# Attention scores exponentiated in PSUM instead of in a moved SBUF row, with the freed SBUF given to three load rings

## The chip, the cores and the metric

The kernel runs on one core of one Trainium2 chip. The metric is the device time of one execution in microseconds, as the median of several executions. Beside it there is one profiled execution with its own time and trace, from which all durations below come.

## What is computed

The outputs of two independent layers are put side by side: a 32-head softmax attention (A) and an FNet mixing layer (B), both over 2048 tokens of width 1024, all in float32.

```python
qkv = (x @ wqkv).reshape(B, S, 3, H, Dh)          # H = 32 heads, Dh = 32
scores = einsum("bhqd,bhkd->bhqk", q, k) * Dh ** -0.5
p = softmax(scores, axis=-1)
A = einsum("bhqk,bhkd->bhqd", p, v) -> [B, S, D] @ wo
a = einsum("bsd,ed->bse", x, dft_hid_re);  b = einsum("bsd,ed->bse", x, dft_hid_im)
B = einsum("ts,bse->bte", dft_seq_re, a) - einsum("ts,bse->bte", dft_seq_im, b)
return concatenate([A, B], axis=-1)
```

## The kernel before, in words

**Two kinds of TensorE work are interleaved.** The first is the dense products: the query, key and value projections, the two stages of B, and the output projection. Each is computed by a seven-product scheme of block additions, and each operand is split into a rounded part and a remainder, so that one product becomes three matmuls of 128 x 128 by 128 x 512. Such matmuls are called "fills" in the code. They are made in `group` (line 398). Their operands pass through rings of SBUF buffers: `RAW` (loaded tiles), `GR` (a second loaded term that is added or subtracted), `HR` and `LR` (the rounded part and the remainder of a stationary piece, tags `h` and `l`), and numbered slots for moving pieces. `fetch` loads and adds (lines 446, 455, 462), `halves` splits (lines 482, 483, 486).

The second kind is attention, in three streams for each head h:

- **S**: 32 score tiles of 128 queries by 1024 keys. Each is two matmuls into one `psS` tile of PSUM (line 1204). The tile is used only for the row's minimum of the negated scores and for the row's sum of exponentials. For h = 0, VectorE takes the negated maximum from PSUM (`tensor_reduce`, line 1214), and ScalarE exponentiates in PSUM, in place, with an accumulated sum (line 1220). For every other head, VectorE copies the negated scores to a row buffer `srow` in SBUF while it takes the minimum (`tensor_scalar` with an accumulated output, line 1212), and ScalarE exponentiates that row in SBUF (line 1218). `srow` has NROW = 2 buffers of 4 KB in each partition.
- **T**: when all S tiles of a head are done, its row minimum is written as two more rows of the query operand (through two small DMAs), and the scores are computed again, transposed and already shifted: 64 matmuls of 128 x 512 into `psT` (line 1335), each followed by a ScalarE exponential into SBUF (line 1339).
- **V**: three blocks of matmuls for each head, after 5, 10 and 16 of its 16 key blocks (`ENDS`), which multiply the exponentials by the values (line 1354).

PSUM has room for two `psS` tiles, two `psT` tiles and two `psD` (`pd`) tiles, the last for fills and V. The rings `psS_r` and `psT_r` say who must be done before a tile is written again: in `scores`, for h > 0, the list `users` of a `psS` tile holds the matmuls and the VectorE operation `b`, while the ScalarE operation `e` belongs to `ruse`, the list of the row buffer. For h = 0 both are in `users`.

**The order of all engines is fixed by a planner** inside the kernel. It plays the program through with a cost for each operation (`MOVE` 1.23, `MAX` 1.22, `ES` 1.31 for the S exponential, `ET` 0.64 for the T exponential, and so on) and emits instructions in that order; each engine's queue then runs in order on the chip. At each free moment of TensorE it chooses: a V block before the others (held back by at most `PATIENCE` 0.5 while an S or T matmul is about to be ready, or while ScalarE has less than `STOCK` 1.8 of work), then S and T, where S may run ahead of T by at most `LEAD`; if none of these is ready, or attention is ahead of its share, the next fill (line 1468). An attention matmul counts as ready `LATE` (0.25; `SLATE`, also 0.25, for S) after the planned end of what it waits for, on top of a latency of 0.1. On ScalarE, T exponentials go before S exponentials; on VectorE, the S operation goes before most of the dense work, the evacuations of the value blocks excepted.

**Stages.** Up to some 180 us there are only fills, whose loads use a ring of raw buffers of their own (`ahead`, line 604, 10 buffers tagged `er`). Attention then runs beside the fills until shortly after 2770 us. The output projection (`behind`, `project`) comes last: it needs the attention output of all heads, its first load waits for the last head's store (list `over`), and its loads use rings of their own, 9 raw tiles and 5 second terms (line 1070), in SBUF that attention has given up.

Of the kernel before, what the change touches and what calls it, by code (L numbers as in the profile page):

```python
# [8 lines left out]
F32 = mybir.dt.float32  # L9
F32R = mybir.dt.float32r  # L10
AF = mybir.ActivationFunctionType
ALU = mybir.AluOpType
# [4 lines left out]
P = 128  # L17
# [5 lines left out]
NS = S // P  # L23
NB = 512
NPT = 24
NROW = 2
NE = 4
NLOW = 5
ENDS = (0, 5, 10, 16)
# [188 lines left out]
def kernel(  # L218
# [114 lines left out]
    def att_low():  # L333

        att()
        return late["atl"]
# [5 lines left out]


    MM, PV, SWITCH, TINY = 0.2272, 0.86, 0.30, 0.17
    ES, ET = 1.31, 0.64
    MOVE = 1.23
    MAX, EVAC, CAST, BIT = 1.22, 0.685, 0.415, 0.275
    SUB = 1.31
    ISSUE = 0.46

    LATE, SLATE = 0.25, 0.25
    HB = 0
    ACAST = 0.63
    RES = 400
# [47 lines left out]
                k += 1  # L402
        frees.append(finish(lambda: box["ps"], o))

    RAW, HR, LR, GR, ER = Ring(5), Ring(3), Ring(3), Ring(3), Ring(NE)
    slots = [[] for _ in range(40)]

    def take_slot(i):
# [83 lines left out]
    def piece(terms, store=None):  # L492

        box = {}
        raw, made, users = fetch([P, 4, P], terms, store)
        (o0, u0), (o1, u1) = HR.take(), LR.take()

        def tile_of(key):
            def get():
                if key not in box:  # L500
                    box[key] = parts.tile([P, 4, P], F32R, name=key, tag=key, bufs=3)
                return box[key]
            return get

        h, l = tile_of("h"), tile_of("l")
        made = halves(raw, made, users, h, l, (o0, o1), (u0, u1), (HR, LR))
        both = Both(u0, u1)
        return Piece(h, l, made, both)
# [66 lines left out]
    def qkv():  # L575
# [25 lines left out]
            }[p]()  # L601

        XS, WV, X, u3 = {}, {}, {}, {}
        ahead = (Ring(10), RAW, lambda shape, name, n: vp.tile(shape, F32, name="er", bufs=10) if name == "raw" else pre.tile(shape, F32, name="raw", tag="raw", bufs=5), [])
        within = where[0]

        def load_x(x, k):
# [458 lines left out]
    def behind():  # L1066

        over.extend(o for h in o_st for o in h)
        for i in range(20, 28):
            slots[i] = list(over)  # L1070
        where[0] = (Ring(9), Ring(5), lambda shape, name, n: op_pool().tile(shape, F32, name=name, tag=name, bufs=n), over)
        spare[0] = True

    over = []
# [91 lines left out]
    psS_r, psT_r, pt_r, vt_r, rt_r, ot_r = Ring(2), Ring(2), Ring(NPT), Ring(2), Ring(1), Ring(2)  # L1166
    small = {n: Ring(b) for n, b in (("st", 2), ("nm", 2), ("lh", 2), ("tw", 1))}
    qx_r = Ring(1)
    row_r = Ring(NROW)
    got = {}  # L1170
    Tops, Sops = {}, {}
    exp_of = {}
# [5 lines left out]
    def scores(h):  # L1178
        ST = {}
        sold, suse = small["st"].take()  # L1180
        maxes, exps = [], []
        if h:
            xold, xuse = qx_r.take()

            def load_x():
                att()
                g, r0 = divmod(h, 4)
                nc.sync.dma_start(f(QX[0])[0 : 3 * DH], qk_d[2 * g][0][r0 * DH : r0 * DH + DH].rearrange("d i c -> (d i) c"))

            got[h, "x"] = op("SP", ISSUE, load_x, [*xold, *qk_st[2 * (h // 4)][0], *(att_gate if h == 1 else [])], [xuse], -2, 192)  # L1190
        for n, (qt, c) in enumerate([(k % 4, k // 4) for k in range(8)] + [divmod(k, 2) for k in range(8, 32)]):
            old, users = psS_r.take()
            own = h > 0 and qt < 4
            box = {}
            if h:
                rold, ruse = row_r.take()

            def mm(n=n, qt=qt, c=c, box=box, own=own):
                if n == 0:
                    ST["negm"] = sm.tile([P, 2, NS], F32, name="negm", bufs=2)  # L1200
                    ST["sums"] = sm.tile([P, 2, NS], F32, name="sums", bufs=2)
                box["p"] = p = psS.tile([P, 1024], F32, name="psS")
                for i in range(2):
                    nc.tensor.matmul(  # L1204
                        p[:, i * NB : i * NB + NB], (QX[0] if own else QS[h % 2])[:, qt * P : qt * P + P],
                        KS[h % 2][:, c * 1024 + i * NB : c * 1024 + i * NB + NB], start=True, stop=True,
                    )

            def mx(qt=qt, c=c, box=box):
                if h:  # L1210
                    box["s"] = att_low().tile([P, 1024], F32, name="srow", bufs=NROW)
                    nc.vector.tensor_scalar(box["s"], box["p"], -1.0, None, op0=ALU.mult, op1=ALU.min, accum_out=ST["negm"][:, c, qt : qt + 1])  # L1212
                    return
                nc.vector.tensor_reduce(out=ST["negm"][:, c, qt : qt + 1], in_=box["p"], axis=AX.X, op=ALU.max, negate=True)

            def ex(qt=qt, c=c, box=box):
                if h:
                    nc.scalar.activation(box["s"], box["s"], AF.Exp, scale=-1.0, bias=ST["negm"][:, c, qt : qt + 1], accum_out=ST["sums"][:, c, qt : qt + 1])  # L1218
                    return
                nc.scalar.activation(box["p"], box["p"], AF.Exp, bias=ST["negm"][:, c, qt : qt + 1], accum_out=ST["sums"][:, c, qt : qt + 1])  # L1220

            a = op("PE", 2 * MM, mm, [*old, *([got.get((h, "x"))] if own else [got.get((h, 0, qt // 4)), got.get((h, "z"))]), got.get((h, 1, 2 * c)), got.get((h, 1, 2 * c + 1))],
                   [users, xuse] if own else [users])
            b = op("DVE", MOVE if h else MAX, mx, [a] + (sold if n == 0 else []) + (rold if h else []), [users, suse, *([ruse] if h else [])], 0)
            e = op("ACT", ES, ex, [b], [ruse if h else users, suse], 0)
            exp_of[a] = e
            maxes.append(b)
            exps.append(e)
            Sops.setdefault(h, []).append(a)
            streams["S"].append((a, h, n))  # L1230
            if n == 5 and h:
                sums(h - 1)

        nold, nuse = small["nm"].take()
        lold, luse = small["lh"].take()
        box = {}

        def nmin():
            ST["nm"] = sm.tile([P, NS], F32, name="nm", bufs=2)
            nc.vector.tensor_reduce(out=ST["nm"], in_=ST["negm"].rearrange("p c n -> p n c"), axis=AX.X, op=ALU.min)  # L1240

        def high():
            box["l"] = sm.tile([P, 2, NS], F32R, name="lh", bufs=2)
            nc.vector.tensor_reduce(out=box["l"][:, 0], in_=ST["negm"].rearrange("p c n -> p n c"), axis=AX.X, op=ALU.min)

        def low():
            return nc.vector.tensor_tensor(out=box["l"][:, 1], in0=ST["nm"], in1=f(box["l"])[:, 0], op=ALU.subtract)

        b = op("DVE", TINY, high, maxes + lold, [luse, suse], -2)
        a = op("DVE", TINY, nmin, maxes + nold, [nuse, suse], -2)  # L1250
        c = op("DVE", TINY, low, [a, b], [nuse, luse], -2, two=True)
        def across():
            box["t"] = sm.tile([P, 2 * NS], F32, name="lt", bufs=2)
            nc.vector.transpose(box["t"], f(box["l"]).rearrange("p i s -> p (i s)"))

        d = op("DVE", TINY, across, [b, c], [luse], -2)

        put = op("SP", ISSUE, lambda: nc.sync.dma_start(m_d[h].rearrange("i (g p) -> g i p", g=4), box["t"]), [d], [luse], -3, 32)
        moved = [op("SP", ISSUE, lambda: nc.sync.dma_start(f(QS[h % 2])[96:98, :], m_d[h].rearrange("(i q) p -> i (q p)", i=2)), [put], [], -3, 16)]
        mine[h] = (ST, suse, nuse, exps, moved)  # L1260
# [154 lines left out]
    while nf < len(fills) or any(place[n] < len(s) for n, s in streams.items()):  # L1415
# [18 lines left out]
        for n, (o, h, k) in heads.items():  # L1434
            if o.left:
                continue
            ready = o.ready + (SLATE if n == "S" else LATE)
            if n == "V":
                ready = max(ready, room)
            if ready > pl.now:  # L1440
                times.append(ready)
                continue
            if n == "V":

                near = any(m in heads and heads[m][0].left == 0 and heads[m][0].ready + LATE < pl.now + NEAR and not (m == "S" and held) for m in "ST")
                if (near or stock < STOCK) and pl.now < o.ready + PATIENCE:
                    times.append(o.ready + PATIENCE)
                    continue
            rank = {"V": 0, "T": 1, "S": 0.5 if stock > SFIRST else 1.5}[n]
            if n == "S" and "T" in heads and heads["T"][0].left == 0:  # L1450
                th, tk = heads["T"][1:]
                lead = k / 33.0 * SST + 16 * (h - th - 1) - tk / 4
                if lead > LEAD:
                    continue
                if lead > 0:
                    rank = 2
            ok.append((rank, n))
# [67 lines left out]
```

## Time and profile before

| what | value |
|---|---|
| median of 3 executions | 2960.72 us (2960.04 to 2961.28) |
| the profiled execution, its own time | 2957.99 us |
| its span, from the first to the last instruction | 2956.1 us |
| mean granted TensorE clock | 1.0 |
| DMA, mean over the span | 189 GB/s |
| last S matmul starts at | 2689.7 us |

How to read the lines shown below: a group's row gives line, engine, operation, tile written <- tiles read, shapes and count, then the busy time in us and the mean duration of one in ns, then the engine's idle time just before and what ended it. A row of the timeline gives start and duration in us, then the instruction and how many of its kind were merged (x2), and in brackets the idle time before it and what ended it. Matmuls are pipelined and their ends are modelled, so the distance between two starts says more than a matmul's duration. A row of the windows gives the stretch, its length, and then busy time and count of PE, PEld (weight loads), DVE (VectorE), ACT (ScalarE) and POOL (GpSimd), the granted clock, the DMA share and GB/s.

### The profile page before, as it was taken

To read this page: it belongs to the slowest core of one execution; us is meant where nothing else is said; L and a number is where in the kernel's file an instruction comes from. 1 tells how busy PE (TensorE), PEld (TensorE's weight loads), DVE (VectorE), ACT (ScalarE), POOL (GpSimd) and SP (SyncE) were. 2 spreads that over 40 slices of the span, in tenths; PEclk is the share of its full clock that TensorE was granted. 3 is DMA by queue.
4 is the path that set the end of the run, shared out by engine and by line. 5 is a ranking of instruction groups with operands and counts; after the bars stand their busy time and mean duration, and the time that the engine had idled before them with its cause. 6 is when DMAs were issued, how large, how long until landed. Compare 5 with 4: busy or idle time off the path is not lost.

```text
span 2956.1 us, 45723 instructions
## 1 busy us (share of the span) xinstructions
PE 2940.3 (99%) x14912; PEld 2145.2 (73%) x14912; DVE 2345.2 (79%) x4198; ACT 2300.3 (78%) x4314; POOL 860.8 (29%) x672
## 2 busy tenths in 40 slices
PE   9999999999999999999999999999999999999999
PEld 7887677776777777777777777777777777677787
DVE  6779788688877877787778888888777888887585
ACT  4348888888898888888888888898888888887421
POOL 2313236222212322221112343332112443442142
PEclk9999999999999999999999999999999999999999
DMA  9975669666626655554535775555434775565662
GB/s 350 355 231 165 191 186 300 215 213 232 205 64 198 206 151 160 174 180 146 155 93 162 229 242 154 174 161 161 118 109 135 238 250 175 167 179 177 233 220 104
DMA packets 376581, 558.59 MB, mean 189 GB/s; under 512 B 111100, under 2 KB 111100, under 8 KB 376220
## 3 DMA queue, kind: packets, MB, share of 16 engines
q1 hardware_dynamic: 376344, 555.68, 59.6%
q8 instruction: 118, 1.93, 0.3%
q14 instruction: 119, 0.97, 0.1%
HBM read 402.42 MB, written 153.11 MB: 188 GB/s over the span
## 4 chain that ended last, share of the span: by engine, by line
PE 98%; DVE 1%; ACT 1%; DMA 0%; POOL 0%; issue 0%; SPq 0%; DVEq 0%; POOLq 0%
PE pd L398 44%; PE psT L1335 16%; PE psS L1204 16%; PE pd L1354 15%; PE psT L398 7%; DVE srow L1212 1%; ACT srow L1218 0%; ACT pt L1339 0%; DMA er<-in_xa 0%; DMA g<-in_ct 0%; DVE h L483 0%; POOL slot L486 0%; POOL l L486 0%; ACT ptl L1339 0%; DVE l L486 0%
## 5 line engine op out<-in xcount | busy, mean ns | idle before, releaser
L1212 DVE TENSOR_SCALAR_CACHE_REDUCE srow<-psS 128x1024 f32<-128x1024 f32 x992 | 1203.2, 1220 | 168.3 <-ACT srow L1218 135.3
L1218 ACT ACTIVATE srow<-srow,negm 128x1024 f32<-128x1024 f32 x992 | 1198.2, 1216 | 6.8 <-DVE srow L1212 6.6
L398 PE MATMUL pd<-slot,h 128*128 128x512 f32 x3384 | 1169.9, 390 | 0.5 <-DVE h L483 0.5
L1339 ACT ACTIVATE pt<-psT 128x512 f32<-128x512 f32 x1618 | 925.9, 645 | 262.3 <-PE psT L1335 226.9
L1335 PE MATMUL psT<-qs,ks 128*128 128x512 f32 x2048 | 793.7, 394 | 1.7 <-ACT pt L1339 1.5
L398 PEld LDWEIGHTS pd<-slot,h 128*128 128x128 f32 x3384 | 635.2, 188 | 136.5 <-issue 1.7
L398 PE MATMUL pd<-slot,l 128*128 128x512 f32 x1692 | 659.6, 390 | 0.9 <-POOL l L486 0.7
L1335 PEld LDWEIGHTS psT<-qs,ks 128*128 128x128 f32 x2048 | 381.5, 188 | 139.4 <-issue 42.8
L1204 PE MATMUL psS<-ks,qs 128*128 128x512 f32 x1552 | 470.4, 391 | 1.0 <-DVE srow L1212 0.8
L486 POOL TENSOR_TENSOR l<-raw,h 128x512 fp32r<-128x512 f32 x152 | 197.2, 1297 | 758.9 <-DVE h L483 349.6
L1354 PE MATMUL pd<-pt,vt 128*32 128x512 f32 x3236 | 394.5, 594 | 0.0
L462 POOL TENSOR_TENSOR raw<-raw,g 128x512 f32<-128x512 f32 x211 | 273.0, 1300 | 376.5 <-DVE raw L462 96.2
L398 PEld LDWEIGHTS pd<-slot,l 128*128 128x128 f32 x1692 | 317.6, 188 | 69.2 <-POOL l L486 1.6
L1204 PEld LDWEIGHTS psS<-ks,qs 128*128 128x128 f32 x1552 | 290.5, 188 | 64.8 <-DVE srow L1212 3.0
L1339 ACT ACTIVATE ptl<-psT 128x512 f32<-128x512 f32 x430 | 249.0, 641 | 106.1 <-PE psT L1335 90.1
L486 POOL TENSOR_TENSOR slot<-raw,slot 128x512 fp32r<-128x512 f32 x154 | 199.0, 1298 | 380.9 <-DVE l L486 97.6
L1218 ACT ACTIVATION_READ_ACCUMULATOR srow<-srow,negm 128x1 f32 x992 | 259.7, 262 | 0.0
L1354 PEld LDWEIGHTS pd<-pt,vt 128*32 128x32 f32 x3236 | 102.0, 110 | 187.4 <-issue 177.3
L398 PE MATMUL pd<-slot,slot 128*128 128x512 f32 x768 | 194.7, 390 | 0.0
L483 DVE CAST h<-raw 128x512 fp32r<-128x512 f32 x321 | 146.6, 458 | 25.9 <-PE pd L398 19.2
L398 PEld LDWEIGHTS pd<-slot,slot 128*128 128x128 f32 x768 | 144.2, 188 | 31.0
L1354 PE MATMUL pd<-ptl,vt 128*32 128x512 f32 x860 | 164.2, 595 | 0.0
(126 smaller groups left out, 2262.6 us busy)
## 6 DMA issues: line engine op xcount, KB each, us to landing
raw<-in_ct SPq DMA_DIRECT2D x224, 256.0 KB
g<-in_ct SPq DMA_DIRECT2D x128, 256.0 KB
qk_d<-e SPq DMA_DIRECT2D x52, 512.0 KB
qs<-qk_d SPq DMA_DIRECT2D x128, 192.0 KB
ks<-qk_d SPq DMA_DIRECT2D x128, 192.0 KB
raw<-ab_d SPq DMA_DIRECT2D x96, 256.0 KB
c<-u_d SPq DMA_DIRECT2D x88, 256.0 KB
g<-ab_d SPq DMA_DIRECT2D x80, 256.0 KB
```

The source lines that it names most:

```text
L398: nc.tensor.matmul(box["ps"], a[1]((a[0].hi, a[0].lo)[u]()), b[1]((b[0].hi, b[0].lo)[v]()), start=k == 0, stop=k == n - 1)
L462: return (nc.gpsimd if e == "POOL" else nc.vector).tensor_tensor(out=dest(), in0=dest() if a is None else a.get(), in1=other["q"] if "q" i ...
L483: return nc.vector.tensor_copy(hi(), raw())
L486: return (nc.gpsimd if e == "POOL" else nc.vector).tensor_tensor(out=lo(), in0=raw(), in1=f(hi()), op=ALU.subtract)
L1204: nc.tensor.matmul(p[:, i * NB : i * NB + NB], (QX[0] if own else QS[h % 2])[:, qt * P : qt * P + P], KS[h % 2][:, c * 1024 + i * NB : c * ...
L1212: nc.vector.tensor_scalar(box["s"], box["p"], -1.0, None, op0=ALU.mult, op1=ALU.min, accum_out=ST["negm"][:, c, qt : qt + 1])
L1218: nc.scalar.activation(box["s"], box["s"], AF.Exp, scale=-1.0, bias=ST["negm"][:, c, qt : qt + 1], accum_out=ST["sums"][:, c, qt : qt + 1])
L1335: nc.tensor.matmul(box["p"], KS[h % 2][:, t * P : t * P + P], QS[h % 2][:, j * NB : j * NB + NB], start=True, stop=True)
L1339: nc.scalar.activation(box["t"], box["p"], AF.Exp)
L1354: nc.tensor.matmul(po["p"][j * DH : j * DH + DH, :], VT[h][:, k, :], box["t"], start=(k == t0), stop=(k == t), tile_position=(0, j * DH),)
```

## The change

For h > 0 the S tiles are now treated like those of h = 0: VectorE takes the negated maximum of the PSUM tile, ScalarE exponentiates in PSUM in place, and the `psS` tile belongs to both until ScalarE is done. The row buffers are gone (8 KB in each partition). That space goes to one more raw buffer (5 to 6), one more second term (3 to 4), and one more rounded part and remainder (3 to 4 each). Since these rings are larger, the raw ring of the first stage has 8 buffers for 10, and those of the output projection have 6 for 9 and 4 for 5. The planner's cost of an S exponential is 1.24 for 1.31, and S uses the same `LATE` as T.

```diff
-NROW = 2
+NRAW, NHL, NG = 6, 4, 4
...
-    ES, ET = 1.31, 0.64
-    MOVE = 1.23
+    ES, ET = 1.24, 0.64
...
-    LATE, SLATE = 0.25, 0.25
+    LATE = 0.25
...
-    RAW, HR, LR, GR, ER = Ring(5), Ring(3), Ring(3), Ring(3), Ring(NE)
+    RAW, HR, LR, GR, ER = Ring(NRAW), Ring(NHL), Ring(NHL), Ring(NG), Ring(NE)
...
-        ahead = (Ring(10), RAW, lambda shape, name, n: vp.tile(shape, F32, name="er", bufs=10) if name == "raw" else pre.tile(shape, F32, name="raw", tag="raw", bufs=5), [])
+        ahead = (Ring(8), RAW, lambda shape, name, n: vp.tile(shape, F32, name="er", bufs=8) if name == "raw" else pre.tile(shape, F32, name="raw", tag="raw", bufs=NRAW), [])
...
-        where[0] = (Ring(9), Ring(5), lambda shape, name, n: op_pool().tile(shape, F32, name=name, tag=name, bufs=n), over)
+        where[0] = (Ring(6), Ring(4), lambda shape, name, n: op_pool().tile(shape, F32, name=name, tag=name, bufs=n), over)
...
             def mx(qt=qt, c=c, box=box):
-                if h:
-                    box["s"] = att_low().tile([P, 1024], F32, name="srow", bufs=NROW)
-                    nc.vector.tensor_scalar(box["s"], box["p"], -1.0, None, op0=ALU.mult, op1=ALU.min, accum_out=ST["negm"][:, c, qt : qt + 1])
-                    return
                 nc.vector.tensor_reduce(out=ST["negm"][:, c, qt : qt + 1], in_=box["p"], axis=AX.X, op=ALU.max, negate=True)
 
             def ex(qt=qt, c=c, box=box):
-                if h:
-                    nc.scalar.activation(box["s"], box["s"], AF.Exp, scale=-1.0, bias=ST["negm"][:, c, qt : qt + 1], accum_out=ST["sums"][:, c, qt : qt + 1])
-                    return
                 nc.scalar.activation(box["p"], box["p"], AF.Exp, bias=ST["negm"][:, c, qt : qt + 1], accum_out=ST["sums"][:, c, qt : qt + 1])
...
-            b = op("DVE", MOVE if h else MAX, mx, [a] + (sold if n == 0 else []) + (rold if h else []), [users, suse, *([ruse] if h else [])], 0)
-            e = op("ACT", ES, ex, [b], [ruse if h else users, suse], 0)
+            b = op("DVE", MAX, mx, [a] + (sold if n == 0 else []), [users, suse], 0)
+            e = op("ACT", ES, ex, [b], [users, suse], 0)
```

More of the change, by code (lines that the diff above doesn't have):

```diff
@@ L500, in get @@
                 if key not in box:
-                    box[key] = parts.tile([P, 4, P], F32R, name=key, tag=key, bufs=3)
+                    box[key] = parts.tile([P, 4, P], F32R, name=key, tag=key, bufs=NHL)
                 return box[key]
@@ L1168 @@
     qx_r = Ring(1)
-    row_r = Ring(NROW)
     got = {}
@@ L1194, in scores @@
             box = {}
-            if h:
-                rold, ruse = row_r.take()
             def mm(n=n, qt=qt, c=c, box=box, own=own):
@@ L1209, in mx @@
             def mx(qt=qt, c=c, box=box):
-                if h:
-                    box["s"] = att_low().tile([P, 1024], F32, name="srow", bufs=NROW)
-                    nc.vector.tensor_scalar(box["s"], box["p"], -1.0, None, op0=ALU.mult, op1=ALU.min, accum_out=ST["negm"][:, c, qt : qt + 1])
-                    return
                 nc.vector.tensor_reduce(out=ST["negm"][:, c, qt : qt + 1], in_=box["p"], axis=AX.X, op=ALU.max, negate=True)
             def ex(qt=qt, c=c, box=box):
-                if h:
-                    nc.scalar.activation(box["s"], box["s"], AF.Exp, scale=-1.0, bias=ST["negm"][:, c, qt : qt + 1], accum_out=ST["sums"][:, c, qt : qt + 1])
-                    return
                 nc.scalar.activation(box["p"], box["p"], AF.Exp, bias=ST["negm"][:, c, qt : qt + 1], accum_out=ST["sums"][:, c, qt : qt + 1])
@@ L1436 @@
                 continue
-            ready = o.ready + (SLATE if n == "S" else LATE)
+            ready = o.ready + LATE
             if n == "V":
```

## The prediction

> **What bounds the kernel now.** I read the busy times of the page first, then TensorE's timeline at its two ends, then who TensorE waited for, and only then ScalarE and VectorE.
>
> ```profile
> PE 2940.3 (99%) x14912; PEld 2145.2 (73%) x14912; DVE 2345.2 (79%) x4198; ACT 2300.3 (78%) x4314; POOL 860.8 (29%) x672
> ```
>
> ```profile
> 7.17 0.80 PE L398 MATMUL psT<-slot,h 128*128 128x512 f32 x1 [7.17 <-ACT slot L482]
> ...
> 2943.54 5.60 PE L398 MATMUL pd<-slot,slot 128*128 128x512 f32 x24
> 2948.98 2.88 PE L398 MATMUL psT<-slot,slot 128*128 128x512 f32 x12
> ```
>
> ```profile
> L1354 PE MATMUL pd<-pt,vt 128*32 128x512 f32 x3236 | 394.5, 594 | 0.0
> ...
> L1354 PE MATMUL pd<-ptl,vt 128*32 128x512 f32 x860 | 164.2, 595 | 0.0
> ```
>
> A busy share of 99% could be an artefact, since ends are modelled. So I count the work. 24 matmuls take 2948.98 - 2943.54 = 5.44 us, 0.2267 each. Of the 14912 matmuls 3236 + 860 = 4096 belong to the value blocks (V); the other 10816 cost 10816 x 0.2267 = 2452 us. A V block of 40 matmuls takes 4.63 us more than its neighbours explain (the rows are below: from 1412.59 to 1417.67 are 5.08 us, less two matmuls of 0.2267), so 4096 / 40 x 4.63 = 474 us. TensorE needs 2926 us; it runs from 7.17 to 2948.98 + 12 x 0.2267 = 2951.7, which is 2944.5. Some 18 us are lost inside the run, no more. **This is the ceiling of any gain**, and the change removes no matmul.
>
> [...]
>
> ```profile
> PE psS L1204 <- DVE srow L1212: 1.0, 3, 0.6
> PE pd L398 <- POOL l L486: 0.7, 2, 0.5
> ```
>
> What the change touches costs TensorE almost nothing today: it waited 1.0 us in all for a score tile's release, and 0.7 us for a remainder of a piece. So the larger rings for raw tiles, second terms and pieces remove a wait that is hardly there: **I take 0 for them**, with 5 us as the most (the losses inside the run that may be late operands).
>
> The time can then only change if attention falls behind, because the output projection needs all heads. So the question is what bounds attention. That is ScalarE:
>
> ```profile
> 1411.60 1.26 ACT L1218 ACTIVATE srow<-srow,negm 128x1024 f32<-128x1024 f32 x1
> 1412.64 0.30 ACT L1218 ACTIVATION_READ_ACCUMULATOR srow<-srow,negm 128x1 f32 x1
> 1412.74 1.19 ACT L1339 ACTIVATE ptl<-psT 128x512 f32<-128x512 f32 x2
> 1413.69 1.27 ACT L1218 ACTIVATE srow<-srow,negm 128x1024 f32<-128x1024 f32 x1
> ...
> 1414.82 1.26 ACT L1218 ACTIVATE srow<-srow,negm 128x1024 f32<-128x1024 f32 x1
> ...
> 1417.87 0.60 ACT L1339 ACTIVATE ptl<-psT 128x512 f32<-128x512 f32 x1 [1.69 <-PE psT L1335]
> ```
>
> One score exponential and two transposed ones go round in 1413.69 - 1411.60 = 2.09 us with no gap. The gap comes at the V block: ScalarE uses up what it had in stock and then stands still for 1.69 us.
>
> **The change, part by part.** *VectorE's operation.* It took 1220 ns with the move and takes 1221 without:
>
> ```profile
> L1212 DVE TENSOR_SCALAR_CACHE_REDUCE srow<-psS 128x1024 f32<-128x1024 f32 x992 | 1203.2, 1220 | 168.3 <-ACT srow L1218 135.3
> L1218 ACT ACTIVATE srow<-srow,negm 128x1024 f32<-128x1024 f32 x992 | 1198.2, 1216 | 6.8 <-DVE srow L1212 6.6
> ```
>
> ```profile
> L913 DVE TENSOR_TENSOR e<-slot,pd 128x512 f32<-128x512 f32 x126 | 86.3, 685 | 46.1 <-PE pd L398 44.8 <-DMA g<-ab_d 0.2
> ...
> L1214 DVE TENSOR_REDUCE negm<-psS 128x1 f32<-128x1024 f32 x32 | 38.7, 1221 | 6.9 <-PE psS L1204 6.7
> ...
> L1220 ACT ACTIVATE psS<-psS,negm 128x1024 f32<-128x1024 f32 x32 | 34.8, 1088 | 26.9 <-DVE negm L1214 26.8
> ```
>
> So 0. VectorE also loses a wait: 135 of its idle us came from a row buffer that ScalarE still held. That wait does not vanish; it moves to TensorE's side, because the tile in PSUM now stays taken instead.
>
> *ScalarE's operation.* The means are 1216 and 1088 ns, 0.13 less from PSUM, but a duration under load contains overlap with the one before. What counts is the step to the next start:
>
> ```profile
> 211.14 1.09 ACT L1220 ACTIVATE psS<-psS,negm 128x1024 f32<-128x1024 f32 x1 [0.61 <-DVE negm L1214]
> 212.15 0.19 ACT L1220 ACTIVATION_READ_ACCUMULATOR psS<-psS,negm 128x1 f32 x1
> 212.96 1.09 ACT L1220 ACTIVATE psS<-psS,negm 128x1024 f32<-128x1024 f32 x1 [0.61 <-DVE negm L1214]
> ```
>
> The accumulator is read 1.01 us after the start from PSUM and 1.04 after it from SBUF (1412.64 - 1411.60). I take 0.03 us saved for each tile, 32 x 0.03 = 1.0 us a head, because the ScalarE queue is full most of the time and the step is then what is paid; 0.13, or 4.2 us a head, is the other end.
>
> [...]
>
> *The stay in PSUM.* This is where it costs. Today a tile is given back after VectorE's 1.22 us; then it will be held until its exponential is done. The rows of h = 0 show the new regime alone, with no transposed exponentials between: ScalarE's starts are 212.96 - 211.14 = 1.82 us apart though it idles 0.61 before each, so the two tiles limit, and each is taken for 3.64 us. In steady state ScalarE wants a tile every 2.09 us, 4.18 for two. **The pipe still fits, with 4.18 - 3.64 = 0.54 us to spare.** VectorE's other operations last 0.69 us (the row of line 913), so one in the way can eat all of this and 0.15 more; the mean over all moments of arrival is small. I take 0.03 us for each of the 26 tiles of a head that don't drain through a V block: 0.8 us a head. The bounds are 0 (every delay within the 0.54) and 0.1 a tile, 2.6 a head.
>
> *The edge of a V block.* Here is TensorE around the block of the ScalarE rows above:
>
> ```profile
> 1411.00 0.62 PE L1204 MATMUL psS<-ks,qs 128*128 128x512 f32 x2
> ...
> 1412.59 0.39 PE L1335 MATMUL psT<-qs,ks 128*128 128x512 f32 x1
> 1412.90 0.62 PE L1354 MATMUL pd<-ptl,vt 128*32 128x512 f32 x1
> ...
> 1417.34 0.50 PE L1335 MATMUL psT<-qs,ks 128*128 128x512 f32 x1
> 1417.67 1.09 PE L1204 MATMUL psS<-ks,qs 128*128 128x512 f32 x4
> ```
>
> The score tile of 1411.00 is the one exponentiated at 1414.82. The tile two before it is exponentiated at 1411.60 and ends near 1412.8. With two tiles in PSUM and no rows in SBUF, the matmul of 1411.00 has to wait for that, and for the planner's 0.1 + 0.25 of caution: 1413.1, by which time the V block has begun. So only one score exponential is in stock behind the two transposed ones, and ScalarE runs dry 1414.82 - 1413.69 = 1.13 us earlier. Against this, with no score matmul about to be ready the planner has no reason to hold the block back. Its last exponentials end at 1411.6, so it could start at about 1412.2 instead of 1412.9, and give 0.6 back. That leaves 0.5 to 0.6 a block. Queued behind the block on TensorE are the next score and transposed matmuls, and ScalarE waits for these. I count two such blocks a head; in the one that ends a head the score stream is held by `LEAD` and by the reload of the keys anyway. So 1.1 us a head, with 0 and 3 x 1.13 = 3.4 as bounds.
>
> *The slack at the end.* A later end of attention is not paid at once, since fills take TensorE's free time meanwhile; it is paid when there are none left that don't need attention's output.
>
> ```profile
> 2774.79 0.32 SPq L1385 DMA_DIRECT2D o_d<-ot  x1
> ```
> ```profile
> 2788.44 1.29 POOL L486 TENSOR_TENSOR slot<-raw,slot 128x512 fp32r<-128x512 f32 x1 [5.21 <-DMA raw<-o_d]
> ```
> ```profile
> 2799.38 2.88 PE L398 MATMUL psT<-slot,slot 128*128 128x512 f32 x12
> ```
>
> The last head is stored at 2774.79, the first operands of the projection are split by 2788.44 + 1.29 = 2789.7, and its first matmul runs at 2799.38, after the last other fill. Attention may slip by 9.7 us, say 10, free of charge.
>
> *The smaller rings.* Eight raw buffers for ten in the first stage, six and four for nine and five in the projection: 0 in the sum, since the second term and piece rings of the first stage grow and the projection's last operands come well ahead. If that cover fails, I bound it by one load-to-split time at the start of the projection, 2789.7 - 2774.8 = 15 us, of which half at most, 8 us, would be new.
>
> **The sum.** For a head: -1.0 + 0.8 + 1.1 = +0.9 us (from -4.2 to +5.0). For 31 heads: +28 us (from -130 to +155). Less 10 of slack: **+18 us**. The profiled execution of 2957.99 us would become 2976; it lies 2.7 below the median of 2960.72, so the median would become 2979.
>
> **The rivals.** *Not slower.* The two tiles suffice: if the stay at the V edge and the late VectorE operations together cost less than ScalarE saves plus 10 / 31 = 0.3 us a head, attention ends early enough and TensorE's work sets the end, 2961. For it: the 0.54 us to spare, and the upper price of ScalarE's gain. Against it: the exponential that is missing from the stock at each V edge. *Faster.* The fuller rings close part of the 18 us, by 5 to 8: 2954. Against it: the 0.7 us of waits on pieces. *The full edge.* V blocks don't come earlier, and two blocks a head lose 1.13 each: 2.26 + 0.8 - 1.0 = 2.1, x 31 = 64, less 10: +54, 3015. *VectorE late.* The planner lets a dense operation onto VectorE just ahead of a score tile again and again, 0.1 us a tile on top of the full edge: 2.26 + 2.6 - 1.0 = 3.9, x 31 = 120, less 10: +110, 3071. ScalarE's rows would then show gaps within the steady stretches. [...]
>
> **How the numbers follow.** My forecast, 2967 to 2996 with 2979 as its value: 0.40. Not slower (2961): 0.27. Full edge (3015): 0.18. VectorE late (3071): 0.10. Faster (2954): 0.05. About 0.2%, 6 us, is what a measurement can tell from no change here. Slower by more: 0.40 + 0.18 + 0.10 = 0.68; within it: 0.27; faster: 0.05. The range leaves out the far half of the full edge, VectorE late, and what is faster than 2955: 2955 to 3035. The likeliest case alone has 2967 to 2996.
>
> **What would show it.** Right: TensorE back to back until the fills that need no attention run out, then a hole of some 20 us before the first matmul of the projection, with the last head's store at about 2803; ScalarE's idle time at V blocks 0.5 us longer, with steady stretches of 2.06 us a turn and no gaps. The forecast is wrong if the last store comes within 10 us of 2775 (not slower), if ScalarE idles between V blocks (VectorE late), or if TensorE's holes lie elsewhere: in the first 180 us or inside the projection, which would be the smaller rings.

## The result, and the profile after

The changed kernel takes 2953.5 us against 2960.0 (medians of 13 executions each), a ratio of 0.9978 (95% interval 0.997 to 0.9986): 6.5 us **faster**, a small gain but clear of the spread, where 18 us slower was forecast. The profiled execution has a span of 2949.8 us for 2956.1. The busy times of the page, and its groups of the score path and of the transposed exponentials:

```profile
PE 2935.9 (100%) x14912; PEld 2145.8 (73%) x14912; DVE 2322.0 (79%) x3198; ACT 2276.8 (77%) x4315; POOL 866.6 (29%) x679
...
L1206 DVE TENSOR_REDUCE negm<-psS 128x1 f32<-128x1024 f32 x1024 | 1240.7, 1220 | 218.3 <-PE psS L1200 211.5
L1209 ACT ACTIVATE psS<-psS,negm 128x1024 f32<-128x1024 f32 x1024 | 1201.4, 1173 | 74.1 <-DVE negm L1206 71.1
L1328 ACT ACTIVATE pt<-psT 128x512 f32<-128x512 f32 x1618 | 960.8, 680 | 262.2 <-PE psT L1324 258.5
```

VectorE's operation costs what it did (1220 ns in the mean, before and after). Its wait for a row buffer (135 us of idle time) has become a wait for score matmuls (211 us), and ScalarE now waits 74 us, nearly all of it for VectorE: 30 of them in the first head, as before, 40 at value blocks, and 4 in the steady stretches between. Hardly any of this reaches TensorE, which waited 1.0 us for the release of score tiles before and waits 0.8 now:

```profile
PE psS L1200 <- ACT psS L1209: 0.8, 2, 0.6
```

Where most of the time was won shows in the windows from 236 to 322 us, an early stretch in which attention and fills run side by side: first the kernel before, then the changed one.

```profile
236.00:322.00 86.00, 82.97 (x392) 59.91 (x391) 77.75 (x155) 76.53 (x144) 38.48 (x30) 1.00 0.63 208
```
```profile
236.00:322.00 86.00, 85.31 (x416) 64.84 (x415) 75.19 (x116) 74.59 (x142) 43.32 (x34) 1.00 0.69 227
```

In the same 86 us TensorE has 416 matmuls instead of 392. At 0.2267 each, 24 matmuls are 5.4 us, most of the gain. They are fills: those of line 398 (397 after) go from 172 to 198, while attention has two matmuls fewer. The timeline of TensorE in the kernel before, within this stretch:

```profile
315.19 0.61 PE L1335 MATMUL psT<-qs,ks 128*128 128x512 f32 x2
316.77 0.49 PE L1335 MATMUL psT<-qs,ks 128*128 128x512 f32 x1 [0.97 <-ACT pt L1339]
317.62 0.50 PE L398 MATMUL pd<-slot,h 128*128 128x512 f32 x1 [0.36 <-DVE h L483]
317.96 0.40 PE L1335 MATMUL psT<-qs,ks 128*128 128x512 f32 x1
318.87 0.50 PE L1335 MATMUL psT<-qs,ks 128*128 128x512 f32 x1 [0.51 <-ACT pt L1339]
```

The holes stand before attention matmuls and are put down to ScalarE. But what is missing is the fills that stand between such matmuls everywhere else; the one fill in these rows waits for its cast. The loads of fill operands run further ahead in the changed kernel: by 300 us, 86 loads into raw buffers have been issued, and 82 in the kernel before. The DMA queue's own waits don't show this as plainly. Loads into a raw buffer (line 446, afterwards 445) wait until GpSimd has made the remainder and so given the buffer back. In the stretch this wait is short in the changed kernel, but as long as before in the run of the next section that has the sixth raw buffer alone and wins nearly as much; so it can't be what the gain is read from. Before, after, and with six raw buffers alone:

```profile
SPq L446 <- POOL slot L486: 16.2, 10, 7.1
```
```profile
SPq L445 <- POOL slot L485: 3.5, 4, 1.1
```
```profile
SPq L445 <- POOL slot L485: 17.6, 12, 8.3
```

Over the whole run I count TensorE's lost time from its timeline: the start of a matmul, less what all before it need (0.2267 for each, and for V blocks 0.1075 for each matmul and 0.33 for each block: in both traces blocks of 40 take 4.63 us and blocks of 48 take 5.49, in the median). The first 6 to 7 us of it pass before the first matmul. Rounded to 0.1 us:

```
up to (us)                    240    330    600   1700   2600   end
before                        9.0   15.3   17.7   23.1   26.9  27.7
changed kernel                9.6   10.7   14.2   18.9   21.0  21.3
PSUM, old rings               9.5   14.8   17.4   23.8   30.7  31.0
PSUM, 6 raw buffers only      9.5   11.1   13.8   19.7   24.1  24.4
```

The difference of 6.4 us between the first two rows at the end is the gain (6.3 in the spans). Between 240 and 330 us the kernel before loses 6.3 us and the changed one 1.1; that is most of it.

### The profile page after: what moved, and what is told of

It reads as the page before. It is cut to its first block, busy times and chain, and to the rows that moved or that the text cites. A ratio compares the mean times of both kernels' runs of the same rounds, so it can differ in the third digit from the quotient of the medians.

```text
span 2949.8 us, 45545 instructions
## 1 busy us (share of the span) xinstructions
PE 2935.9 (100%) x14912; PEld 2145.8 (73%) x14912; DVE 2322.0 (79%) x3198; ACT 2276.8 (77%) x4315; POOL 866.6 (29%) x679
## 4 chain that ended last, share of the span: by engine, by line
PE 97%; DMA 1%; DVE 1%; issue 0%; ACT 0%; POOL 0%; SPq 0%; POOLq 0%; ACTq 0%; DVEq 0%
PE pd L397 44%; PE psT L1324 16%; PE psS L1200 16%; PE pd L1343 15%; PE psT L397 7%; DMA er<-in_xa 0%; DVE negm L1206 0%; DMA m_d<-lt 0%; DMA c<-u_d 0%; POOL raw L461 0%; ACT psS L1209 0%; DMA raw<-in_wv 0%; DVE slot L485 0%; DVE slot L482 0%; DVE raw L461 0%
## 5 line engine op out<-in xcount | busy, mean ns | idle before, releaser
L1206 DVE TENSOR_REDUCE negm<-psS 128x1 f32<-128x1024 f32 x1024 | 1240.7, 1220 | 218.3 <-PE psS L1200 211.5
L1209 ACT ACTIVATE psS<-psS,negm 128x1024 f32<-128x1024 f32 x1024 | 1201.4, 1173 | 74.1 <-DVE negm L1206 71.1
L1328 ACT ACTIVATE pt<-psT 128x512 f32<-128x512 f32 x1618 | 960.8, 680 | 262.2 <-PE psT L1324 258.5
L397 PE MATMUL pd<-slot,h 128*128 128x512 f32 x3368 | 1145.6, 390 | 0.0
L1324 PE MATMUL psT<-qs,ks 128*128 128x512 f32 x2048 | 802.1, 395 | 1.8 <-DMA qs<-m_d 1.1
L485 POOL TENSOR_TENSOR l<-raw,h 128x512 fp32r<-128x512 f32 x170 | 219.2, 1290 | 851.5 <-PE psT L1324 348.6
L485 POOL TENSOR_TENSOR slot<-raw,slot 128x512 fp32r<-128x512 f32 x165 | 212.5, 1292 | 401.9 <-DVE slot L482 147.6
L1328 ACT ACTIVATE ptl<-psT 128x512 f32<-128x512 f32 x430 | 260.9, 681 | 81.3 <-PE psT L1324 81.3
L1209 ACT ACTIVATION_READ_ACCUMULATOR psS<-psS,negm 128x1 f32 x1024 | 298.4, 291 | 0.0
```

Source lines behind the costliest of these rows:

```text
L397: nc.tensor.matmul(box["ps"], a[1]((a[0].hi, a[0].lo)[u]()), b[1]((b[0].hi, b[0].lo)[v]()), start=k == 0, stop=k == n - 1)
L485: return (nc.gpsimd if e == "POOL" else nc.vector).tensor_tensor(out=lo(), in0=raw(), in1=f(hi()), op=ALU.subtract)
L1324: nc.tensor.matmul(box["p"], KS[h % 2][:, t * P : t * P + P], QS[h % 2][:, j * NB : j * NB + NB], start=True, stop=True)
L1328: nc.scalar.activation(box["t"], box["p"], AF.Exp)
```

## The experiments

In the sessions of these runs the kernel before had medians of 2959.1 to 2960.2 us.

**Which part carries it.** The changed kernel with every ring as before (the lines on `ahead` and the projection are shortened):

```diff
-NRAW, NHL, NG = 6, 4, 4
+NRAW, NHL, NG = 5, 3, 3
-ahead: 8 er buffers;   projection: Ring(6), Ring(4)
+ahead: 10 er buffers;  projection: Ring(9), Ring(5)
```

> Scores exponentiated in PSUM, but every ring as before (5 raw, 3 second terms, 3 pieces, 10 and 9/5). Rings theory (the gain is fill operands that come in time at the start of attention): the TensorE holes of 5.8 us between 250 and 320 us come back, 2958 to 2961. Score theory (the gain comes from how scores are released and exponentiated): they stay away, 2952 to 2955. Accident theory (any change of order moves the holes): anything between, with holes at other places.

Measured: 2961.4 us, ratio to before 1.0007 (0.9999 to 1.0016). The whole gain is gone, and the holes are back:

```profile
249.88 0.72 PE L1200 MATMUL psS<-ks,qx 128*128 128x512 f32 x2 [0.33 <-ACT psS L1209]
250.44 0.63 PE L1324 MATMUL psT<-qs,ks 128*128 128x512 f32 x2
251.59 0.73 PE L1200 MATMUL psS<-ks,qx 128*128 128x512 f32 x2 [0.52 <-ACT psS L1209]
252.16 0.90 PE L1324 MATMUL psT<-qs,ks 128*128 128x512 f32 x2
253.66 0.74 PE L1200 MATMUL psS<-ks,qx 128*128 128x512 f32 x2 [0.59 <-ACT psS L1209]
```

Score and transposed matmuls follow each other with no fill between, and each score tile then waits for a tile in PSUM. The score path with its own planner's cost is worth nothing by itself, and costs nothing that can be told. The three rings were then given back one at a time, with the changed kernel's smaller rings in the first stage and in the projection:

```diff
-NRAW, NHL, NG = 6, 4, 4
+NRAW, NHL, NG = 5, 4, 3      # e5;   6, 3, 3: e6;   5, 3, 4: e7
```

> The changed kernel with 5 raw buffers and 3 second terms as before, but 4 stationary pieces. If the fourth piece is what keeps fills ready (TensorE's holes of the old rings are before score matmuls, when no fill is at hand): 2953 to 2956 and no holes at 250, 1680 and 2400 us. If raw tiles or second terms do it: 2958 to 2962.

> The changed kernel with 6 raw buffers, but 3 pieces and 3 second terms. Piece theory: 2957 to 2962, holes back. Raw theory: 2953 to 2956.

> The changed kernel with 4 second terms, but 5 raw buffers and 3 pieces. Piece and raw theory: 2957 to 2962, holes back. Second-term theory: 2953 to 2956.

Measured: 4 pieces 2961.4 us, **6 raw buffers 2953.9 us**, 4 second terms 2962.5 us. The raw theory is the one that came true. The sixth raw buffer alone is worth 2961.4 - 2953.9 = 7.5 us, and the other two nothing that can be told from the median. Between 240 and 330 us the three lose 5.7, 1.6 and 4.5 us, and the old rings 5.3. The run with six raw buffers has 413 matmuls in the stretch from 236 to 322 us (193 of them fills, where the old rings have 177), and 86 loads into raw buffers issued by 300 us, where the old rings have 83:

```profile
236.00:322.00 86.00, 85.64 (x413) 64.21 (x412) 76.92 (x115) 73.92 (x141) 47.07 (x37) 1.00 0.68 229
```

**More of it, and the rings that were made smaller.**

```diff
-NRAW, NHL, NG = 6, 4, 4
+NRAW, NHL, NG = 9, 3, 3      # e11
+NRAW, NHL, NG = 6, 3, 3      # e12, with 10 er buffers and Ring(9), Ring(4) in the projection
```

> Scores in PSUM, all the freed space given to raw tiles: 9 raw buffers, 3 pieces, 3 second terms. Raw theory with more to gain: 2948 to 2953, the holes left over at 510, 1680 and 2400 us gone. If six already suffice: 2952 to 2956.

> Scores in PSUM, 6 raw buffers, 3 pieces and 3 second terms as in the run with six raw buffers, but with 10 raw buffers in the first stage and 9 in the projection. If the smaller rings of the first and the last stage cost nothing, as predicted: within 2 us of that run (2953.9), the same time lost up to 200 us and after 2790 us. If they cost: 2 to 8 us less than it.

Measured: nine raw buffers 2952.1 us (ratio to before 0.9973, 0.9963 to 0.9984; that of the change is 0.9978, so these two can't be told apart), and six with the old raw rings of the first stage and of the projection 2953.85, the same as with the smaller ones (2953.88). Nine and six ran in the same session: 2951.1 to 2953.2 against 2952.3 to 2956.0, so three more raw buffers may be worth another 1.8 us. Of the holes named, those at 1680 and 2400 us are gone with nine, and the one at 510 us stays. Six raw buffers bring most of the gain, and the smaller raw rings cost nothing, as predicted.

**Does the raw buffer help with the moved rows too?** The 2 KB for it had to come from another ring, so each run has a control.

```diff
-NE = 4                       # e9, e10: 3 results
+NE = 3
-RAW, HR, LR, GR = Ring(5), Ring(3), Ring(3), Ring(3)
+RAW, HR, LR, GR = Ring(6), Ring(3), Ring(3), Ring(3)      # e10
+RAW, HR, LR, GR = Ring(5), Ring(3), Ring(3), Ring(2)      # e13
+RAW, HR, LR, GR = Ring(6), Ring(3), Ring(3), Ring(2)      # e14
```

> The kernel before with 3 buffers for 4 in the ring of evacuated results (NE), which frees 2 KB a partition: the control for the next run. 2960 to 2968: a smaller ring can only hold evacuations back. With the holes of the kernel before at 250 and 315 us.

> The same with a sixth raw buffer in the 2 KB, moved rows kept. Raw theory: 5 to 8 us below the control, the holes at 250 and 315 us gone, so the gain was to be had without exponentiating in PSUM. If the sixth raw buffer only helps the order that PSUM scores make: within 3 us of the control.

> The kernel before with 2 second terms for 3, which frees 2 KB a partition without touching the ring of results: the control for the next run. Since a fourth second term was worth nothing, the loss of the third may cost little: 2960 to 2975.

> The same with a sixth raw buffer in the 2 KB, moved rows kept. Raw theory: 4 to 8 us below the control, the holes of TensorE at 250 and 315 us smaller. If a sixth raw buffer helps only together with scores in PSUM: within 3 us of the control, or slower.

Measured: 2996.9 for the control with three result buffers and 3015.4 with six raw ones; 2992.3 for the control with two second terms and 2992.5 with six raw ones. Both controls were far slower than I expected: one buffer taken from either ring costs 32 to 37 us, and these rings then set the time. So the total does not answer the question, and both runs with six raw buffers miss what the raw theory expected: one equals its control, the other is 18.4 us slower. The lost time speaks against the raw theory here. Between 240 and 330 us it is 6.8 us in the control with three result buffers and 6.5 with the sixth raw buffer, 3.2 and 2.6 in the other pair; with scores in PSUM the same buffer took it from 5.3 to 1.6. By 300 us, 81 and 83 loads into raw buffers had been issued in the first pair. Up to 1000 us the lost time went from 54.5 to 71.8 us in that pair, and from 30.6 to 21.7 in the other, where the later stages take the gain away again. **This stays open**: with the moved rows there was no 2 KB to be had without a large loss, so no run shows the sixth raw buffer by itself there. What is shown is its worth in the kernel that exponentiates in PSUM.

**The planner's cost of a score exponential.** The diff also changes `ES` from 1.31 to 1.24, and I had not priced it.

```diff
-    ES, ET = 1.24, 0.64
+    ES, ET = 1.31, 0.64      # e2, changed kernel;  1.20: e15
-    ES, ET = 1.31, 0.64
+    ES, ET = 1.24, 0.64      # e8, kernel before
```

> The changed kernel with only the planner's cost of a score exponential back at 1.31. Rings and score theory: 2952 to 2955, within 2 us of the changed kernel, since the chip does the same work and no ring changes. Accident theory: 3 to 8 us off, with new holes of TensorE.

> The kernel before, moved rows and all, with only the planner's cost of a score exponential lowered from 1.31 to 1.24. Pace theory (TensorE never waits, so attention advances as fast as the written order says): the last value block ends some 20 to 45 us earlier than 2773. The time can't gain from that. ScalarE's step on rows is 1.13 against a planned 1.24 - 0.15 = 1.09, so TensorE will wait for it where fills run out: 2958 to 2975. If ScalarE itself sets the pace, the last value block stays within 5 us of 2773 and the time within 2 us.

> The changed kernel with the planner's cost of a score exponential at 1.20 for 1.24, which is 0.04 less than ScalarE's step of 1.09 plus the 0.15 of overlap. Matched-cost theory (a cost told too low makes TensorE wait in its queue, one told too high lets attention end late): holes before score and transposed matmuls within the attention stage, 31 x 32 x 0.04 = 40 us at most, 2965 to 2990. If the cost only sets the pace: attention ends earlier and the time stays within 2 us of 2953.

Measured: 2983.3 us at 1.31, 2961.8 at 1.20, and the kernel before with 1.24 takes 2988.1. All are slower, and by two different mechanisms; none of the three times lies in a range that I had written down. At 1.31 the order written out gives attention fewer turns than ScalarE could take. Attention's last store and the first projection matmuls:

```profile
2806.84 0.33 SPq L1374 DMA_DIRECT2D o_d<-ot  x1
```
```profile
2815.85 3.23 PE L397 MATMUL psT<-slot,slot 128*128 128x512 f32 x6 [10.60 <-ACT slot L481]
```

The store is 43.9 us later than in the changed kernel (2762.9), the fills have run out, and TensorE stands for 10.6 us. With 1.24 on moved rows ScalarE is slower than it was told (a step of 1.13 against 1.24 - 0.15 = 1.09; the planner lets the next ScalarE operation begin 0.15 before the end of one). TensorE's lost time is 57.9 us instead of 27.7, with its first large hole in the timeline before a score matmul:

```profile
482.22 2.37 PE L1204 MATMUL psS<-ks,qx 128*128 128x512 f32 x4 [2.85 <-DVE srow L1212]
```

The pace theory expected attention to end 20 to 45 us earlier there. It ended later, at 2791.7 instead of 2774.8: the holes added 30.2 us, so the order by itself gained 13. At 1.20 the holes cost 10.2 us of lost time (31.5 for 21.3) and 8.3 us of time. So 1.24 is the best of three values tried for this form, and 1.31 the better of two for the moved rows: the form and its cost had to change together.

**Is attention's end the bound?** One more ScalarE activation of 32 columns behind each score exponential, told to the planner at 0.11:

```diff
+                if 0 < h < 6:        # e3;   0 < h < 32: e4
+                    return nc.scalar.activation(box["p"][:, 0:32], box["p"][:, 0:32], AF.Exp)
-            e = op("ACT", ES, ex, [b], [users, suse], 0)
+            e = op("ACT", ES + (0.11 if 0 < h < 6 else 0.0), ex, [b], [users, suse], 0)
```

> The changed kernel with one more ScalarE activation of 32 columns behind each score exponential of heads 1 to 5, which spoils their sums of exponentials' tile but not the sums. It costs ScalarE about 0.12 us each, 32 x 5 x 0.12 = 19 us. If ScalarE sets the pace of attention and the end has some 15 us of slack: last value block about 19 us later, time 2953 to 2960. If attention's pace set the time: 2972.

> The same extra activation in heads 1 to 31: 31 x 32 x 0.12 = 119 us of ScalarE. Slack theory: attention ends some 119 us later, less 15 us that are free, 2953 + 104 = 3057 (3035 to 3075), with TensorE's holes in the last stretch before the projection. If ScalarE had room of its own beside attention: below 2970.

Measured: 2962.7 us and 3076.2 us (the second a single execution). Both are above what I expected; the step was mis-sized. ScalarE's timeline in the run with all heads:

```profile
1398.95 1.11 ACT L1209 ACTIVATE psS<-psS,negm 128x1024 f32<-128x1024 f32 x1
1399.95 0.22 ACT L1209 ACTIVATION_READ_ACCUMULATOR psS<-psS,negm 128x1 f32 x1
1400.20 0.18 ACT L1211 ACTIVATE psS<-psS 128x32 f32<-128x32 f32 x1
1400.30 1.08 ACT L1330 ACTIVATE pt<-psT 128x512 f32<-128x512 f32 x2
1401.25 1.11 ACT L1209 ACTIVATE psS<-psS,negm 128x1024 f32<-128x1024 f32 x1
```

A turn takes 1401.25 - 1398.95 = 2.30 us for 2.05 without it: 0.25, not 0.12. The small activation starts 0.25 us after the accumulator's read, where the transposed one starts 0.09 after it without the small one, and the transposed one follows 0.10 after the small one. With five heads the last store comes at 2779.2, 16.2 us later. TensorE loses only 32.7 - 31.0 = 1.7 us after 2750 us; the 31.0 - 21.2 = 9.8 us more than the changed kernel's up to there (24.9 against 14.2 by 600 us) it lost in the loaded stretch itself, where ScalarE is slower than told. With all heads the store comes at 2900.4, 137.5 us later, and the time is 123 us longer; 83.9 - 21.2 = 63 us of it TensorE lost before 2750 us, most of it in steps a little longer than 0.2267. This fits two prices. **Time that TensorE loses between attention's matmuls is paid at once. A delay that the order itself contains is free up to about 14 us and paid in full beyond**: 137.5 - 63 - 14 = 60, and 146.2 - 83.9 = 62 us were lost after 2750 (the 14 are read from the run at 1.31, below). With five heads the order's own delay is 16.2 - 9.8 = 6.4 us, and was free.

## Why the prediction was wrong

**Two steps failed. The first gave the forecast its sign: attention was to end 28 us later, by +0.9 us a head, and to cost 18.** It ended 11.9 us earlier (last store at 2762.9 for 2774.8). The run with the old rings has this attention alone, with its planner's cost, and its ratio to before is 1.0007: the term of +18 us measured about +2, within the spread. The two costs in it, 0.8 + 1.1 us a head, came to 0.5 of ScalarE's idle time, and ScalarE saved 1.3 instead of 1.0 (both below). And the sum was not what sets the end of attention: with the cost at 1.31 and the same work on the chip, the last store came at 2806.8. That this is near the forecast of 2803, and the 2983.3 us of that run near 2979, is chance: only the cost told to the planner made that delay.

**The second: "I take 0 for them, with 5 us as the most", for the larger rings.** The sixth raw buffer is worth 7.5 us in the kernel with scores in PSUM, and it is the whole gain within the spread. I had sized it by TensorE's list of waits, 0.7 us on pieces. That list names what the next instruction in the queue waited for. Where no fill is ready in its plan, the planner puts an attention matmul in its place, and the wait is booked under that matmul's release. The list is also too short. In the rows at 315 us the second transposed matmul of the first row starts near 315.42 and would be followed after 0.2267 us; the next starts at 316.77, so 1.12 us were lost, of which the profile shows 0.97 as idle. My count of 18 us lost inside the run was near the trace's 27.7 - 7.2 = 20.5, but I did not ask where it lay: 6.3 of it lay between 240 and 330 us. Nor is all of it waiting. Steps longer than they need by over 0.02 us add up to 12 us inside the run; most of the rest is that beside attention an ordinary step is 0.2276 in the mean (180 to 2770 us), and not 0.2267 as in the projection. By which wait the sixth buffer lets the loads run ahead is not shown; that they do, and that fills then stand where the holes were, is.

**The ceiling** held: the change won 6.5 us, less than 18. So did the reading that 99% busy leaves little.

**ScalarE's shorter step** was right. The timeline of the changed kernel around a V block, ScalarE first and then TensorE:

```profile
1401.39 1.22 ACT L1209 ACTIVATE psS<-psS,negm 128x1024 f32<-128x1024 f32 x1
1402.39 0.34 ACT L1209 ACTIVATION_READ_ACCUMULATOR psS<-psS,negm 128x1 f32 x1
1402.48 1.22 ACT L1328 ACTIVATE pt<-psT 128x512 f32<-128x512 f32 x2
1403.44 1.24 ACT L1209 ACTIVATE psS<-psS,negm 128x1024 f32<-128x1024 f32 x1
...
1407.53 1.29 ACT L1209 ACTIVATE psS<-psS,negm 128x1024 f32<-128x1024 f32 x1
...
1412.99 0.60 ACT L1328 ACTIVATE ptl<-psT 128x512 f32<-128x512 f32 x1 [2.46 <-PE psT L1324]
```
```profile
1407.25 0.62 PE L1200 MATMUL psS<-ks,qs 128*128 128x512 f32 x2
1407.70 0.39 PE L1324 MATMUL psT<-qs,ks 128*128 128x512 f32 x1
1408.02 0.62 PE L1343 MATMUL pd<-ptl,vt 128*32 128x512 f32 x1
```

A turn takes 1403.44 - 1401.39 = 2.05 us for 2.09. The step is 0.04 shorter, where I took 0.03. The source and the result moved to PSUM together here, and no run separates the two. It is the planner's cost that turns this into time: with the same step on the chip, the runs at 1.31 and 1.20 are 29.8 and 8.3 us slower.

**The stay in PSUM and the edge of a V block** were rightly seen and mis-sized. The steady rows shown have no gap, as 0.54 us to spare promised. At the block ScalarE now stands for 2.46 us instead of 1.69. In these rows the block begins 1408.02 - 1407.53 = 0.49 us after the last transposed exponentials made way, where it was 1412.90 - 1411.60 = 1.30: it comes earlier, as argued, and by somewhat more. In sum: ScalarE's idle time before attention's exponentials was 262 + 106 + 7 + 27 = 402 us before and is 262 + 81 + 74 = 417 after. The numbers are the idle times in the groups' rows; those not shown so far are these, two of before and one of after. That is 15 us more over 31 heads, 0.5 us a head net, where I had put 0.8 + 1.1.

```profile
L1339 ACT ACTIVATE pt<-psT 128x512 f32<-128x512 f32 x1618 | 925.9, 645 | 262.3 <-PE psT L1335 226.9
...
L1339 ACT ACTIVATE ptl<-psT 128x512 f32<-128x512 f32 x430 | 249.0, 641 | 106.1 <-PE psT L1335 90.1
```

```profile
L1328 ACT ACTIVATE ptl<-psT 128x512 f32<-128x512 f32 x430 | 260.9, 681 | 81.3 <-PE psT L1324 81.3
```

So a head's sum was about -1.3 + 0.5 instead of +0.9. Over 31 heads that is -25 us, and attention ended 11.9 us earlier; the difference is not accounted for, and the planner's cost moves this end by more than either.

**The slack at the end** was right as a mechanism. In the run at 1.31 the last store is 43.9 us later than in the changed kernel and the time 29.8 longer: 14 us were free. The changed kernel's own slack, by the rows from which I read 10 us in the kernel before, is 2792.95 - 2777.86 = 15.1:

```profile
2776.57 1.29 POOL L485 TENSOR_TENSOR slot<-raw,slot 128x512 fp32r<-128x512 f32 x1 [4.74 <-DMA raw<-o_d]
```
```profile
2792.95 2.88 PE L397 MATMUL psT<-slot,slot 128*128 128x512 f32 x12
```

**What the prediction left out** is the planner's cost. Of the edits that were undone alone it is the one that moves the time most: 29.8 us. I had listed it as part of the change and given it no term.

**The rivals.** "Faster" had the right place (fuller rings close part of the lost time) and the right size (5 to 8 us). I gave it 0.05 on the strength of the list of waits. "Not slower" had the right reason for attention, and neither the full edge nor a late VectorE showed: outside the first head, ScalarE's waits for VectorE lie at V blocks but for 4 us. I had looked for the cost in ScalarE's gaps; that at the V block grew from 1.69 to 2.46 us in the rows shown, at no cost that could be told. The gaps that cost time were TensorE's: the holes at 250 to 254 us, with the old rings, shrank with one more buffer in SBUF (5.3 us lost from 240 to 330 us for 1.6).

## What to carry to other kernels

In a kernel whose order is written out by a planner, as here, TensorE's waits name the instruction that the planner put there, not the one that was missing; look for stretches in which one kind of work is absent, and price rings by how far the loads run ahead there, since the loads' own waits were as long with the ring that helped. A cost given to such a planner is part of the kernel: when an operation changes its form, tell its new step, since a cost 0.04 to 0.07 us off cost 8 to 30 us here, on either side. The tiles held longer cost nothing that could be told here, where their turn (3.64 us) fits into that of ScalarE (4.18), so compare these two times before pricing the waits one by one.

## What I had not expected

In this kernel a ring is worth little above a certain size and very much below it: a sixth raw buffer gave 7.5 us and three more 2 at most, a fourth second term gave nothing, and the third of them (with moved rows) was worth 32 us.

A ScalarE activation of 32 columns on the PSUM tile that the exponential before it had just written cost 0.25 us a turn. An independent one of the same size in SBUF cost 0.12, by the same run's timeline; whether the dependence or the place makes the difference is not shown:

```profile
1408.14 0.24 ACT L1268 ACTIVATE tt<-tt 128x32 f32<-128x32 f32 x1
1408.26 1.10 ACT L1209 ACTIVATE psS<-psS,negm 128x1024 f32<-128x1024 f32 x1
```
